# Sliding-window attention followed by a gated feed-forward layer: a smaller first weight load, batch 0's small steps in another order, and value casts by head into the tile layout

## The chip, the cores and the metric

The kernel runs on one core of a Trainium2 chip. The metric is device time in microseconds (us), as the median of several runs. Five engines of the core work side by side, each on its own queue in its own order: TensorE (PE, matrix products; PEld is its weight load), VectorE (DVE), ScalarE (ACT), GpSimd (POOL) and SyncE (SP). Transfers between HBM and the on-chip memory are issued from POOL's queue or from SP's queue and are carried by 16 DMA engines that all queues share.

## The reference

Eight batches of eight heads, 576 tokens and 64 values per head go through attention in which a query sees the keys within 32 positions, and 8 global tokens see and are seen by everything. The result, laid out as 4608 tokens of 512 values, goes through a feed-forward layer whose nonlinearity is h + sin(alpha h)^2 / alpha.

```python
scores = scale * np.matmul(q, k.transpose(0, 1, 3, 2))
mask = np.abs(pos[:, None] - pos[None, :]) <= window      # window = 32
mask = mask | is_global[:, None] | is_global[None, :]
attn = softmax(np.where(mask, scores, -1e9))
x = (attn @ v).transpose(0, 2, 1, 3).reshape(B * S, H * D)
h = x @ w_in                                              # 512 -> 2048
s = np.sin(alpha * h)
out = (h + s * s / (alpha + 1e-9)) @ w_out                # 2048 -> 512
```

## The kernel before, in words

The order of the work on every engine is the order in which the code is written. The kernel goes through the batches with the attention of one batch beside the second product of the batch before: `phase_a(0)`, then for each batch b `gemm1(b)` (x @ w_in with the nonlinearity) and `phase_a(b + 1, b)`, in which the products of `gemm2(b)` (g @ w_out, line 1220) are spread by hand with `fill(n)` between the steps of batch b + 1's attention. `fill` has nothing to lay into batch 0's attention, which therefore runs alone; that is the start that the change touches.

**Batch 0's attention** is `first_batch` (called in `attention`). The eight heads go in four pairs hp = 0 to 3. For each pair `scores` (line 814) makes the scores in PSUM, ACT takes their exponential (line 822), DVE multiplies the mask in (`cover`, line 831). `denominators(hp)` is 28 matmuls with a weight of ones (line 862 into `zd`), then the logarithm on ACT (`L`, line 772, which writes the tile `L` and issues its copy to `LC` from SP), then a small sum for the global tokens on DVE (`GD`, line 756). `inverse(hp)` is exp(-L) on ACT (`R`, line 779). `first_numerators(hp)` is 28 matmuls with the values `VF` as weights (line 862), 8 for the global rows (line 878) and `normalise`: the product with `R` into `xT` (line 908) and the sum `GN` (line 756) on DVE. In batch 0 the numerators go to PSUM banks `zr` (hp 0 and 2), `zn` (hp 1) and `zd` (hp 3); the denominators of every pair go to `zd`. `set_recip` turns alpha into a column (a PE transpose, line 710, and a DVE copy, line 711) and makes 1/(alpha + 1e-9) from it (`recipT`, lines 712 and 713). `warm(z, n)` (line 569) is n matmuls of 512 columns whose result nobody reads.

In the kernel before, the pairs' loop ends with `denominators(2)`. Then follow on PE: numerators 0, numerators 1, the alpha transpose, denominators 3, numerators 2, one warm matmul, numerators 3, two warm matmuls, and `gemm1(0)`.

**`gemm1(0)`** goes through 16 groups nt of 128 columns of w_in (line 1115). It first makes the chunks 0 to 2 of groups 0 and 1 (which need xT of pairs 0 to 2), then chunk 3 of both, then whole groups. Three PSUM tiles, `zn`, `zr` and `zd`, take turns, so group 3 needs the tile of group 0 back: ACT's sine (line 1162, needs `alphaT`), a square (line 1165 on ACT or 1167 on DVE) and DVE's line 1168 (needs `recipT`) come between. Between the groups PE turns the keys and queries of batch 1 (`turn_lying`, line 630; `H` there is a corner of the tile H2 in which they lie) and the global keys and queries (`turn_kq`, line 726, from the two `gkq` tiles that POOL casts in line 717).

**POOL's queue** issues, in this order: the twelve loads of batch 0's values (line 392), `load_w_in(0, 1)` (line 426), a cast of the global values, a one-element copy (`pace`, line 353) that waits for the first exponential of pair 3, `load_w_in(1, 2)`, keys and queries of batch 1 for pairs 0 and 1 (line 456), `load_w_in(2, 4)`, the same for pairs 2 and 3, a copy that waits for the edge of the value tile, the cast of batch 1's values to a bf16 copy in HBM (`cast_v(1)`, line 334), the two halves of w_out (line 432), the two `gkq` casts, and the cast of batch 2's queries. `load_w_in(lo, hi)` counts quarters of w_in's 2048 columns. A transfer issued from POOL uses one of eight semaphores in turn (DMASW0 to DMASW7), and the instruction that issues it waits until the transfer eight places earlier has landed.

**SP's queue** gathers the global rows of v, k and q (lines 518 and 512), then writes batch 0's four logarithms to `LC`, then loads batch 1's values from their cast copy (`load_v(1)`, line 407, tile `VF`; `vd` is the cast copy), then the global rows beside them (line 414).

The cast copy `vd` of a batch has the layout [token, head, value]. A partition of the value tile takes one token of each of 7 key tiles of 48 tokens, so `load_v` reads 7 pieces of 512 bf16 values for each of 48 partitions, twice.

`cast_one(b, name, h)` casts one head of a later batch; keys go into a copy with the layout [token within a key tile, key tile, head, value] (line 344), queries and values into [token, head, value] (line 346).

Of the kernel before, what the change touches and what calls it, by code (L numbers as in the profile page):

```python
# [249 lines left out]
def kernel(  # L250
# [85 lines left out]
    def cast_one(b, name, h):  # L336

        src = {"qd": q, "kd": k, "vd": v}[name][b, h]
        tiles = name == "kd"
        if h == 0:  # L340
# [7 lines left out]
    def cast_v(b):  # L348
        cast_heads(b, v, "vd")

# [51 lines left out]
    def load_v(b):  # L402

        src = cast[b, "vd"][:].rearrange("(m a) h d -> a m (h d)", a=KT)
        for half in range(2):
            m0 = half * (NT6 - 1)
            nc.sync.dma_start(
                out=VX[b % 2][half * D : half * D + KT].rearrange("p m h d -> p m (h d)"),
                in_=src[:, m0 : m0 + NT6 + 1],
            )  # L410
# [12 lines left out]
    def load_w_in(lo, hi):  # L423
        if lo < hi:
            cols = slice(lo * DFF // 4, hi * DFF // 4)
            nc.gpsimd.dma_start(
# [281 lines left out]

    def set_recip():
        nc.tensor.transpose(out=zo[0][:, 0:NT], in_=arow[:], identity=idf[0:NT, 0:NT])  # L710
        nc.vector.tensor_copy(out=alphaT[:], in_=zo[0][:, 0:NT])
        nc.vector.tensor_scalar(out=recipT[:], in0=alphaT[:], scalar1=1e-9, scalar2=None, op0=ALU.add)  # L712
        nc.vector.reciprocal(out=recipT[:], in_=recipT[:])
# [68 lines left out]
    def attention(b, beside):  # L782
# [136 lines left out]
        def first_batch():  # L919

            for hp in range(NHP):
# [5 lines left out]
                if hp == last:  # L927
                    pace(Es[hp][0:1, 0, 0, 0:1])
                    load_w_in(1, 2)
                    for hps in (early, late):  # L930
                        for w in (1, 0):
                            load_lying(1, w, hps)
                        if hps == early:
                            load_w_in(2, 4)
                    for half in (1, 0):
# [5 lines left out]
                for g in range(2 * (hp > 0)):  # L941
                    cover(hp, g)
                if hp:
                    denominators(hp - 1)
            release_ring()
            for hp in range(2):
                inverse(hp)
                first_numerators(hp)
            set_recip()
            inverse(last - 1)  # L950
            denominators(last)
            first_numerators(last - 1)
            warm(zo[1], 1)
# [4 lines left out]
            warm(zo[1], 2)  # L958
            normalise(last)
            pair["after"].release()  # L960

# [435 lines left out]
```

## Time and profile before

| | us |
|---|---|
| median of 3 runs | 338.68 (338.3 to 339.26) |
| the profiled execution | 338.49 |
| its span, first to last instruction | 336.8 |
| PE busy | 316.2 |
| ACT busy | 277.1 |
| DVE busy | 255.9 |
| POOL busy | 143.7 |

The profile is of one execution. Its own time is 338.49 us; 1.7 us of that lie outside the span of 336.8 us. All times below are counted from the span's start. In a list of groups or of the timeline each row is: start, busy time, engine, line, operation, output<-inputs, shape, count, and in square brackets the idle time of the engine just before, with what ended it. "issue" there means that the engine waited for nothing that the profile shows. In the rows on DMA the last number is the time from issue to landing. In the rows on queues the numbers are packets, megabytes and the time of the packets as a share of 16 engines' time; packets overlap, so shares can exceed 100%.

### The profile page before, as it was taken

The numbers are of one execution on the slowest core, as the hardware profiler recorded it, in microseconds if no ns is written. First come the engines' busy times: TensorE is split into PE (matmuls) and PEld (weight loads), VectorE is DVE, ScalarE is ACT, GpSimd is POOL, SyncE is SP. The second block draws the span as 40 slices with busy tenths as digits, with TensorE's granted clock in tenths as the row PEclk, the third lists the DMA queues.
The fourth block names the chain that finished last, engine by engine and source line by source line (L and its number), as shares of the span: only waits on it lengthen the run. The fifth ranks groups of instructions, "written<-read, shape, count | busy, mean of one in ns | idle before, by whom it ended". The sixth has DMA issues, their size and how long they took to land.

```text
span 336.8 us, 11878 instructions
## 1 busy us (share of the span) xinstructions
PE 316.2 (94%) x4812; PEld 202.8 (60%) x4812; DVE 255.9 (76%) x488; ACT 277.1 (82%) x402; POOL 143.7 (43%) x296
## 2 busy tenths in 40 slices
PE   0778999999999999999999999999999999999993
PEld 0765765577556765667556755676567745665553
DVE  4885896887887788688877788778868888788930
ACT  6775888989998889988998889889898898889611
POOL 7983324349516670666355652487060000004500
PEclk9999999999999999999999999999999999999998
DMA  7999999999989998999969993899999311010232
GB/s 104 114 162 205 186 226 169 152 166 135 181 143 133 190 124 137 94 119 186 151 93 137 172 162 85 131 176 136 132 111 133 65 60 42 1 33 8 73 93 69
DMA packets 141942, 42.01 MB, mean 125 GB/s; under 512 B 126426, under 2 KB 136794, under 8 KB 141882
## 3 DMA queue, kind: packets, MB, share of 16 engines
q0 software_dynamic: 100096, 18.51, 71.1%
q1 hardware_dynamic: 41786, 22.69, 34.1%
q8 instruction: 38, 0.62, 0.8%
q14 instruction: 22, 0.18, 0.2%
HBM read 41.95 MB, written 20.77 MB: 186 GB/s over the span
## 4 chain that ended last, share of the span: by engine, by line
PE 87%; DVE 4%; ACT 3%; issue 2%; DMA 1%; POOL 1%; DVEq 0%; POOLq 0%
PE zo L1220 38%; PE zn L1115 14%; PE zr L1115 11%; PE zd L1115 10%; PE ring L814 4%; PE zd L862 4%; PE zn L862 2%; DVE H L1168 2%; DMA g0k<-in_k_dram,grow 1%; ACT sb L1162 1%; PE zn L814 1%; PE zr L862 1%; DVE recipT L712 1%; DVE s L1167 1%; PE zo L630 1%
## 5 line engine op out<-in xcount | busy, mean ns | idle before, releaser
L1220 PE MATMUL zo<-w_out,H 128*128 128x512 bf16 (+1 forms) x576 | 147.1, 377 | 0.3 <-DVE KX L637 0.3
L1115 PEld LDWEIGHTS <-w_in 128*128 128x128 bf16 x1024 | 100.1, 98 | 43.9 <-issue 8.3
L1220 PEld LDWEIGHTS <-H 128*128 128x128 bf16 x592 | 53.7, 98 | 46.2 <-issue 0.4
L1115 PE MATMUL zn<-xT,w_in 128*128 128x288 bf16 (+1 forms) x384 | 57.7, 290 | 1.6 <-DVE H L1168 1.4
L1115 PE MATMUL zr<-xT,w_in 128*128 128x288 bf16 x320 | 48.0, 288 | 0.3
L1168 DVE SCALAR_TENSOR_TENSOR H<-s,recipT,zn 128x576 bf16<-128x576 bf16 (+1 forms) x48 | 39.4, 822 | 10.4 <-ACT s L1165 6.5
L1162 ACT ACTIVATE sb<-zn,alphaT 128x576 bf16<-128x576 f32 (+1 forms) x48 | 35.7, 743 | 13.7 <-PE zn L1115 13.2
L1115 PE MATMUL zd<-xT,w_in 128*128 128x288 bf16 x320 | 46.3, 288 | 0.3 <-DVE H L1168 0.2
L822 ACT ACTIVATE E<-ring 128x720 bf16<-128x720 f32 x46 | 35.9, 780 | 8.3 <-PE ring L814 7.7
L1167 DVE TENSOR_TENSOR s<-sb 128x576 bf16<-128x576 bf16 (+1 forms) x70 | 32.6, 465 | 12.2 <-ACT sb L1162 12.0
L1165 ACT ACTIVATE s<-sb 128x576 bf16<-128x576 bf16 (+1 forms) x58 | 40.0, 689 | 1.8
L831 DVE TENSOR_TENSOR E<-E,MASKT 128x720 bf16<-128x720 bf16 x64 | 33.5, 529 | 7.6 <-ACT E L822 5.6
L1168 DVE SCALAR_TENSOR_TENSOR H<-s,recipT,zd 128x576 bf16<-128x576 bf16 (+1 forms) x40 | 32.9, 822 | 7.6 <-ACT s L1165 5.0
L1168 DVE SCALAR_TENSOR_TENSOR H<-s,recipT,zr 128x576 bf16<-128x576 bf16 (+1 forms) x40 | 32.9, 822 | 6.6 <-ACT s L1165 5.0
L344 POOL DMA_DIRECT2D kd<-in_k_dram x48 | 31.4, 657 | 10.4 <-issue 8.0
L1162 ACT ACTIVATE sb<-zd,alphaT 128x576 bf16<-128x576 f32 (+1 forms) x40 | 29.6, 740 | 5.2 <-PE zd L1115 5.1
L1162 ACT ACTIVATE sb<-zr,alphaT 128x576 bf16<-128x576 f32 (+1 forms) x40 | 29.6, 740 | 4.3 <-PE zr L1115 4.3
L1210 POOL COPY H<-H 128x11 bf16 (+1 forms) x16 | 7.2, 453 | 57.6 <-DVE H L1168 56.7
L346 POOL DMA_DIRECT2D vd<-in_v_dram x48 | 30.5, 645 | 1.7 <-issue 1.3
L346 POOL DMA_DIRECT2D qd<-in_q_dram x40 | 25.4, 635 | 6.0 <-issue 6.0
L1227 ACT COPY osb<-zo 128x512 f32<-128x512 f32 (+1 forms) x33 | 19.1, 580 | 10.6 <-PE zo L1220 7.0
L814 PEld LDWEIGHTS <-KX 64*64 64x64 bf16 x896 | 15.8, 112 | 19.4 <-issue 19.0
(171 smaller groups left out, 377.7 us busy)
## 6 DMA issues: line engine op xcount, KB each, us to landing
VF<-vd SPq DMA_DIRECT2D x14, 336.0 KB
kd<-in_k_dram POOLq DMA_DIRECT2D x48, 72.0 KB, 4.8
vd<-in_v_dram POOLq DMA_DIRECT2D x48, 72.0 KB, 4.1
qd<-in_q_dram POOLq DMA_DIRECT2D x40, 72.0 KB, 5.5
w_out<-in_moe_w_out_dram POOLq DMA_DIRECT2D x2, 1024.0 KB, 25.7
out_dram<-osb SPq DMA_DIRECT2D x7, 256.0 KB
out_dram<-osb SPq DMA_DIRECT2D x8, 224.0 KB
out_dram<-osb SPq DMA_DIRECT2D x8, 192.0 KB
```

The source lines that it names most:

```text
L344: nc.gpsimd.dma_start(out=dst[:, :, h], in_=src.rearrange("(i a) d -> a i d", a=KT))
L346: nc.gpsimd.dma_start(out=dst[:, h], in_=src)
L814: nc.tensor.matmul(out=z[half * D : (half + 1) * D, t, 0 : G3 * WCOL].rearrange("p (m x c) -> p m x c", x=2, c=60)[:, m % G3, :, c0:c1], l ...
L822: nc.scalar.activation(out=weights(hp, g), in_=z[:, :, 0 : G3 * WCOL], func=AF.Exp, scale=scale)
L831: nc.vector.tensor_tensor(out=Eg, in0=Eg, in1=MASKT[:, None, G3 * g : G3 * (g + 1), :].rearrange("p o m c -> p o (m c)").to_broadcast([P, ...
L862: nc.tensor.matmul(out=nd(hp, key)[t * D : (t + 1) * D, half, :, a - half * CUT : z - half * CUT], lhsT=ones[rows, 0:D] if key else values ...
L1115: nc.tensor.matmul(out=h_part, lhsT=w_in[:, c, nt * P : (nt + 1) * P], rhs=xT[:, c, lo:hi], start=(c == 0), stop=(c == CT - 1), skip_group ...
L1162: nc.scalar.activation(out=sb[:, 0:W], in_=h, func=AF.Sin, scale=alphaT[:, nt : nt + 1])
L1165: nc.scalar.activation(out=s2[:, 0:W], in_=sb[:, 0:W], func=AF.Square)
L1167: nc.vector.tensor_tensor(out=s2[:, 0:W], in0=sb[:, 0:W], in1=sb[:, 0:W], op=ALU.mult)
L1168: nc.vector.scalar_tensor_tensor(out=H2[:, nt, r0 : r0 + W], in0=s2[:, 0:W], scalar=recipT[:, nt : nt + 1], in1=h, op0=ALU.mult, op1=ALU.add,)
L1220: nc.tensor.matmul(out=ops[:, cols], lhsT=H2[:, nt, blk * P : (blk + 1) * P], rhs=w_out[:, nt, cols], start=(nt == 0), stop=(nt == NT - 1) ...
```

## The change

There are three edits. First, `load_w_in` counts eighths instead of quarters; the call `load_w_in(0, 1)`, whose line is the same, now loads the first eighth (256 columns, groups nt = 0 and 1), the second call loads the next three eighths and the third the upper half as before. Second, the small steps of batch 0 are put in another order: `set_recip` is split into `set_alpha` (transpose and copy) and a `set_recip` that is only the two DVE operations and comes behind the last `normalise`; `inverse(0)` comes before `denominators(2)`; `denominators(3)` comes before numerators 1 and 2 and behind one more warm matmul. Third, batch 1's values are cast by eight transfers of one head each, and the cast copy of the values of every batch takes the layout that the keys have, so that `load_v` finds the 7 pieces of a partition side by side.

```diff
-        tiles = name == "kd"
+        tiles = name != "qd"
...
     def cast_v(b):
-        cast_heads(b, v, "vd")
+        for h in range(H):
+            cast_one(b, "vd", h)
...
     def load_v(b):
-        src = cast[b, "vd"][:].rearrange("(m a) h d -> a m (h d)", a=KT)
+        src = cast[b, "vd"][:].rearrange("a m h d -> a m (h d)")
...
     def load_w_in(lo, hi):
-            cols = slice(lo * DFF // 4, hi * DFF // 4)
+            cols = slice(lo * DFF // 8, hi * DFF // 8)
...
-    def set_recip():
+    def set_alpha():
         nc.tensor.transpose(out=zo[0][:, 0:NT], in_=arow[:], identity=idf[0:NT, 0:NT])
         nc.vector.tensor_copy(out=alphaT[:], in_=zo[0][:, 0:NT])
+
+    def set_recip():
...
-                    load_w_in(1, 2)
+                    load_w_in(1, 4)
...
-                            load_w_in(2, 4)
+                            load_w_in(4, 8)
...
+                if hp == last:
+                    inverse(0)
                 if hp:
                     denominators(hp - 1)
             release_ring()
-            for hp in range(2):
-                inverse(hp)
-                first_numerators(hp)
-            set_recip()
-            inverse(last - 1)
+            inverse(1)
+            first_numerators(0)
+            set_alpha()
+            warm(zo[1], 1)
             denominators(last)
-            first_numerators(last - 1)
+            inverse(2)
+            first_numerators(1)
+            first_numerators(2)
             warm(zo[1], 1)
...
             normalise(last)
+            set_recip()
```

**DVE at the end of batch 0's attention, before.** xT is the normalised result, GN and GD are the sums for the global tokens, recipT is 1/(alpha + 1e-9):

```order
L908 TENSOR_TENSOR xT<-zr,R 128x576 [waits PE_49,Activation_49]
L756 TENSOR_REDUCE GN<-zr 128x2x4
L908 TENSOR_TENSOR xT<-zn,R 128x576 [waits PE_49,Activation_49]
L756 TENSOR_REDUCE GN<-zn 128x2x4
L711 COPY alphaT<-zo_125 128x16 [waits PE_49]
L712 TENSOR_SCALAR recipT<-alphaT 128x16 [waits DVE_49]
L713 RECIPROCAL recipT<-recipT 128x16 [waits DVE_49]
L756 TENSOR_REDUCE GD<-zd 128x2x4 [waits Activation_49]
L908 TENSOR_TENSOR xT<-zr,R 128x576 [waits PE_49]
L756 TENSOR_REDUCE GN<-zr 128x2x4
L908 TENSOR_TENSOR xT<-zd,R 128x576 [waits PE_49,Activation_49]
L756 TENSOR_REDUCE GN<-zd 128x2x4
```

The same place of the changed kernel, whose lines are numbered 3 higher here:

```order
L911 TENSOR_TENSOR xT<-zr,R 128x576 [waits PE_49]
L759 TENSOR_REDUCE GN<-zr 128x2x4
L712 COPY alphaT<-zo_125 128x16 [waits PE_49]
L759 TENSOR_REDUCE GD<-zd 128x2x4 [waits Activation_49]
L911 TENSOR_TENSOR xT<-zn,R 128x576 [waits PE_49]
L759 TENSOR_REDUCE GN<-zn 128x2x4
L911 TENSOR_TENSOR xT<-zr,R 128x576 [waits PE_49,Activation_49]
L759 TENSOR_REDUCE GN<-zr 128x2x4
L911 TENSOR_TENSOR xT<-zd,R 128x576 [waits PE_49,Activation_49]
L759 TENSOR_REDUCE GN<-zd 128x2x4
L715 TENSOR_SCALAR recipT<-alphaT 128x16 [waits DVE_49]
L716 RECIPROCAL recipT<-recipT 128x16 [waits DVE_49]
```

The sum GD of pair 3, for which PE's numerators 3 wait (they reuse zd), has moved ahead of pairs 1 and 2, and the two recipT operations have moved from before it to the end of the row. On PE, likewise, denominators 3 now stand behind the alpha transpose and a warm matmul and ahead of numerators 1 and 2.

**POOL's queue from the second w_in load to w_out, before.** H_97 is the place where batch 1's keys and queries lie, seen is the one-element copy:

```order
L426 DMA w_in<-in_moe_w_in_dram 128x4x512 [waits DMASW3_49]
L456 DMA H_97<-in_k_dram 48x4x768 [waits DMASW4_49]
L456 DMA H_97<-in_q_dram 48x4x768 [waits DMASW5_49]
L426 DMA w_in<-in_moe_w_in_dram 128x4x1024 [waits DMASW6_49]
L456 DMA H_97<-in_k_dram 48x4x768 [waits DMASW7_49]
L456 DMA H_97<-in_q_dram 48x4x768 [waits DMASW0_49]
L937 COPY seen<-VF_91 1x1 [waits DVE_49,Pool_49]
L334 DMA vd<-in_v_dram 4608x1x64 [waits DMASW1_49]
L432 DMA w_out<-in_moe_w_out_dram 128x8x512 [waits DMASW2_49]
L432 DMA w_out<-in_moe_w_out_dram 128x8x512 [waits DMASW3_49]
```

In the changed kernel the six loads ahead stand in the same places with the same semaphores, and behind them:

```order
L940 COPY seen<-VF_91 1x1 [waits DVE_49,Pool_49]
L344 DMA vd<-in_v_dram 576x1x64 [waits DMASW1_49]
L344 DMA vd<-in_v_dram 576x1x64 [waits DMASW2_49]
L344 DMA vd<-in_v_dram 576x1x64 [waits DMASW3_49]
L344 DMA vd<-in_v_dram 576x1x64 [waits DMASW4_49]
L344 DMA vd<-in_v_dram 576x1x64 [waits DMASW5_49]
L344 DMA vd<-in_v_dram 576x1x64 [waits DMASW6_49]
L344 DMA vd<-in_v_dram 576x1x64 [waits DMASW7_49]
L344 DMA vd<-in_v_dram 576x1x64 [waits DMASW0_49]
L433 DMA w_out<-in_moe_w_out_dram 128x8x512 [waits DMASW1_49]
L433 DMA w_out<-in_moe_w_out_dram 128x8x512 [waits DMASW2_49]
```

One cast has become eight, so the third to the eighth head now wait for the second w_in load, the four loads of batch 1's keys and queries and the third w_in load to land, and the two halves of w_out wait for the first and the second head's cast instead of for the first two w_in loads.

## The prediction

> **What bounds the kernel now.** I read the page first, then PE's waits behind the start, then PE's timeline in the start, since that is where the order of the small steps lies.
>
> ```profile
> span 336.8 us, 11878 instructions
> ```
> ```profile
> PE zn L1115 <- DVE H L1168: 1.4, 2, 1.0
> ```
> The second row is the largest of PE's waits after 30 us. PE is the bound from there to the end, so whatever the start gives back reaches the end, unless a transfer that doesn't come earlier takes it away. So there are two questions: how much earlier does `gemm1(0)` begin, and what is PE's next tight date? The timeline of PE answers the first:
>
> ```profile
> 15.23 0.38 PE L862 MATMUL zd<-E,ones 56*64 56x120 bf16 x9 [0.68 <-issue]
> ...
> 20.24 0.79 PE L862 MATMUL zd<-E,ones 56*64 56x88 bf16 x28
> ...
> 24.38 0.51 PE L862 MATMUL zd<-E,ones 56*64 56x120 bf16 x16 [1.02 <-issue]
> ...
> 26.78 0.79 PE L862 MATMUL zd<-E,VF 56*64 56x88 bf16 x28 [0.48 <-DVE GD L756]
> ...
> 27.77 1.03 PE L569 MATMUL zo<-ones 128*128 128x512 bf16 x2
> 28.60 1.65 PE L1115 MATMUL zn<-xT,w_in 128*128 128x288 bf16 x6
> 30.04 1.14 PE L1115 MATMUL zr<-xT,w_in 128*128 128x288 bf16 x6
> ...
> 31.50 1.14 PE L1115 MATMUL zd<-xT,w_in 128*128 128x288 bf16 x8
> 33.67 1.14 PE L1115 MATMUL zn<-xT,w_in 128*128 128x288 bf16 x8 [1.03 <-DVE H L1168]
> 34.65 1.14 PE L1115 MATMUL zr<-xT,w_in 128*128 128x288 bf16 x8
> ```
> From denominators 2 (20.24) to `gemm1(0)` (28.60) PE needs 8.36 us, and two gaps lie in them: 1.02 us in the middle of denominators 3, where no instruction is waited for, and 0.48 us ahead of numerators 3, for the sum GD on DVE. Beside the gaps there is pace: the six matmuls from 28.60 to 30.04 start every 240 ns, the eight from 33.67 to 34.65 every 123 ns. The first 16 of `gemm1(0)` take 2.90 us and would take 1.97 at the later pace.
>
> The tight date is found behind the start. The second half of w_out is used first here:
>
> ```profile
> 51.34 1.67 PE L1220 MATMUL zo<-w_out,H 128*128 128x512 bf16 x7 [0.25 <-DVE KX L637]
> ...
> 55.80 0.47 PE L862 MATMUL zd<-E,ones 56*64 56x88 bf16 x28
> ...
> 56.23 2.10 PE L1220 MATMUL zo<-w_out,H 128*128 128x512 bf16 x9
> ```
> and the halves are issued by POOL, and land after the time at the row's end (lists of one issue each):
>
> ```profile
> 25.48 1.34 POOL L432 DMA_DIRECT2D w_out<-in_moe_w_out_dram  x1
> 27.63 0.89 POOL L432 DMA_DIRECT2D w_out<-in_moe_w_out_dram  x1 [0.80 <-DMA w_in<-in_moe_w_in_dram]
> ```
> ```profile
> w_out<-in_moe_w_out_dram POOLq DMA_DIRECT2D x1, 1024.0 KB, 22.9
> ```
> ```profile
> w_out<-in_moe_w_out_dram POOLq DMA_DIRECT2D x1, 1024.0 KB, 28.6
> ```
> The first half lands at 25.48 + 22.9 = 48.4, 2.9 us before its use at 51.34. The second lands at 27.63 + 28.6 = 56.2, and PE begins with it at 56.23, straight behind denominators that began at 55.80. This date has no slack: a PE that comes earlier waits here for w_out, and the start's gain counts only as far as w_out's second half lands earlier too.
>
> **The order of the small steps.** GD of pair 3 comes late because of what stands ahead of it on DVE:
>
> ```profile
> 24.23 2.13 DVE L712 TENSOR_SCALAR recipT<-alphaT 128x16 f32<-128x16 f32 x1
> 26.40 0.25 DVE L713 RECIPROCAL recipT<-recipT 128x16 f32<-128x16 f32 x1
> ...
> 32.23 0.46 DVE L1167 TENSOR_TENSOR s<-sb 128x576 bf16<-128x576 bf16 x1 [3.37 <-ACT sb L1162]
> ```
> The change puts both directly ahead of line 1167, the last of these rows. Even at 2.13 + 0.25 = 2.38 us they fit into the 3.37 us in which DVE waits for ACT, so they cost nothing there; without that cover they would cost up to 2.38. GD now comes two numerators ahead of its use, which ends the 0.48 us. ACT makes R of pair 0 ahead of the logarithm of pair 2; what waits for that is GD of pair 2 and then denominators 3, which come later on PE by numerators 0 and a warm matmul, so I take nothing. The additional warm matmul costs half of what two take from 27.77 to 28.60: 0.41 us.
>
> The gap of 1.02 us is a load of code. The first row is POOL's transfer queue (q0) from 14 to 16 us, around the gap of 0.68 at 15.23; the other two are that queue and the instruction queue (q8) from 22 to 24 us, where one packet of code runs just ahead of the gap of 1.02:
>
> ```profile
> q0 software_dynamic: 1481, 0.18, 144.1%
> ```
> ```profile
> q0 software_dynamic: 318, 0.32, 104.1%
> ...
> q8 instruction: 1, 0.02, 3.0%
> ```
> The pieces in the queue are 0.18 MB / 1481 = 122 bytes ahead of the short gap and 1 KB ahead of the long one. If a code load stands behind the pieces of other queues, their size sets its wait. The first eighth has pieces of 512 bytes where the first quarter has 1 KB. So the gap is between 1.02 (it stays) and nothing; I take the half with the smaller pieces, 0.4 left.
>
> On the rings, the Trainium skill ("DMA: Bandwidth & Descriptors", Queues, rings and completion order) says that an engine drains a whole packet, typically 9 to 17 descriptors, of one ring before it turns to the next. By that rule the code load waits for some 16 pieces, half as long with pieces half as large; the two gaps agree in direction, and nothing here shows the count.
>
> So `gemm1(0)` begins earlier by 0.62 + 0.48 - 0.41 = 0.7 us (0.07 with the gap kept, 1.09 without it). If PE has its later pace by then, 2.90 - 1.97 = 0.93 more; the bounds of the gain are 0.07 and 2.02, and I take 1.3. What is late next is `zn` for group 3 (33.67), which hangs on group 0 and moves along.
>
> The Trainium skill ("TensorE: Matmul & The Clock Gate", What's actually happening) says that PE runs at half rate until it has been busy through one free-running window of about 3.4 us. By that rule the closed gaps bring the full rate a window earlier and the gain is 2.0 rather than 1.1; the trace agrees in that the pace doubles between 30.04 and 31.50, about 4 us behind the last gap.
>
> **The w_in split.** The bytes stay the same. Only the queue can run dry between the smaller first load and the second, whose issue waits for an exponential:
>
> ```profile
> 16.50 0.87 POOL L426 DMA_DIRECT2D w_in<-in_moe_w_in_dram  x1
> ...
> 19.88 0.76 POOL L426 DMA_DIRECT2D w_in<-in_moe_w_in_dram  x1
> ```
> ```profile
> w_in<-in_moe_w_in_dram POOLq DMA_DIRECT2D x1, 512.0 KB, 6.3
> ```
> Half of 6.3 us would land the eighth at 19.65; the next load is issued by 20.64. So the queue is empty for 0 to 1.0 us, and all that stands behind it, w_out last, comes later by as much. I take 0.3, since the queue still has values to carry when the eighth is issued.
>
> **The casts by head.** POOL pays eight issues for one:
>
> ```profile
> L344 POOL DMA_DIRECT2D kd<-in_k_dram x48 | 31.4, 657 | 10.4 <-issue 8.0
> ```
> ```profile
> 23.10 0.57 POOL L456 DMA_DIRECT2D H<-in_q_dram  x1
> ...
> 23.79 2.16 POOL L334 DMA_DIRECT2D vd<-in_v_dram  x1
> ```
> ```profile
> H<-in_q_dram POOLq DMA_DIRECT2D x1, 288.0 KB, 15.1
> ```
> ```profile
> vd<-in_v_dram POOLq DMA_DIRECT2D x1, 576.0 KB, 18.0
> ```
> Eight at 657 ns are 5.3 us for 2.16, but the waits weigh more. The eighth head waits for the last queries, 23.10 + 15.1 = 38.2, and w_out's halves for the first two heads. The cast of the values lands at 23.79 + 18.0 = 41.8 now, so it moves from 38.2 to 41.8, 0.45 us per head. The first head is then done by about 39, w_out is issued within another 1.34 us, and the queue has values until 41.8: it doesn't run empty. If landings are seen late, w_out comes up to 1 us late; I take 0.2. Behind w_out on POOL stand the `gkq` casts:
>
> ```profile
> 36.45 0.61 POOL L717 CAST gkq<-SQ 64x512 bf16<-64x512 f32 x1 [6.63 <-DMA LC<-L]
> ```
> ```profile
> 46.03 0.68 PE L726 MATMUL zo<-identb,gkq 64*64 64x32 bf16 x32
> ```
> Issued about 41.5, they end by 43, ahead of 46.03 less 1.3.
>
> What can bring w_out forward is the new layout. SP's load of the values runs beside w_out. The rows are POOL's queue from 42 to 45 us, alone, then both from 46 to 50:
>
> ```profile
> q0 software_dynamic: 588, 0.60, 121.7%
> ```
> ```profile
> q0 software_dynamic: 471, 0.48, 70.3%
> q1 hardware_dynamic: 470, 0.46, 48.5%
> ```
> ```profile
> VF<-vd SPq DMA_DIRECT2D x14, 336.0 KB
> ```
> Alone, w_out moves 588 / 3 = 196 packets per us; beside 470 packets of SP's it loses 784 - 471 = 313 in 4 us, so one of SP's costs 0.67 / 196 = 3.4 ns. The two loads of a batch are 672 packets of 1 KB: 2.3 us. As 96 packets of 7 KB they cost 0.3 us if the price is per packet, 2.3 if it is per byte. The gain is 0 to 2.0 us. Pieces of 122 bytes moved at 740 per us (1481 in 2 us), an eighth of the bytes at a quarter of the price, which is nearer to the byte; I take 0.8. The later batches' loads gain the same way, but PE waits for none of them.
>
> **The sum.** w_out's second half lands at 56.2 + 0.3 + 0.2 - 0.8 = 55.9. PE is ready for it at 56.2 - 1.3 = 54.9 and waits 1.0 us. Gain: 0.3 us of 338.49, the profiled execution's own time, which is 0.2 under the median of 338.68. That gives 338.2, and on the scale of the median 338.4; I say 338.2, as the gain has more room above than below. A measurement of this kernel can tell about 0.3%, 1.0 us, from no change.
>
> **Rivals.** Faster: the price is per packet, and w_out lands 1.0 us or more earlier, up to 56.2 - 2.0 = 54.2; then the start's 1.1 to 2.0 come through, and the time is 336.5 to 337.5, middle 337.0. For it: the two gaps on PE are real, and the new pieces are seven times larger. Against it: the packet prices above. Chance 0.36.
>
> Slower: POOL stands behind the eight semaphores and the queue runs dry ahead of w_out. A single head's cast takes this long by its row:
>
> ```profile
> kd<-in_k_dram POOLq DMA_DIRECT2D x48, 72.0 KB, 4.8
> ```
> Issued from 38.2 to 38.9, the eighth head would land at 43.7 instead of 41.8: 1.9 us. With 1.0 from the first load and no gain from the layout w_out's second half lands at 59.1. It decides from 57.2 on, where the loss passes 1.0 us, and gives 339.5 to 341.4, middle 340.4. Against it: the queue should still hold values when w_out is issued. Chance 0.17.
>
> The start doesn't get shorter: the code load comes as late as before, the gain is 0.07, and the time stays within 0.3% whatever w_out does up to 57.2. This and my forecast are the same verdict; together 0.47, of which the forecast has 0.3. The forecast's own range is 337.7 to 339.7. The whole range, with half of the fast rival's lower end and some of the slow one's, is 336.7 to 339.8.
>
> **What would show it.** Right: L1115 begins at 27.3 or so; the gap in front of it on GD is gone; a wait of about a microsecond on w_out stands at the first use of its second half, near 55.9; POOL waits on transfers between the heads. The order's part is wrong if the 1.02 us stay or the matmuls keep 240 ns to 30 us. The cap is wrong if w_out lands a microsecond or more ahead of 55.9, or behind 57.2. A wait of PE on `gkq`, on the second w_in load or on the values would be one that I cost at nothing.

## The result, and the profile after

| | before | after |
|---|---|---|
| median | 338.97 us (338.3 to 340.08, 4 runs) | 344.27 us (343.89 to 346.33, 4 runs) |
| the profiled execution, and its span | 338.49, 336.8 | 344.05, 342.4 |

The ratio is 1.0168, with a 95% interval of 1.0138 to 1.0197: slower by 1.7%, outside the predicted range of 336.7 to 339.8.

In the profiled execution the start comes earlier by about what the prediction said, though not by the way that it said. PE's timeline after:

```profile
24.73 0.35 PE L865 MATMUL zn<-E,VF 56*64 56x120 bf16 x9 [1.07 <-issue]
...
28.35 0.90 PE L1122 MATMUL zn<-xT,w_in 128*128 128x288 bf16 x6
...
30.31 1.14 PE L1122 MATMUL zd<-xT,w_in 128*128 128x288 bf16 x8
32.48 1.14 PE L1122 MATMUL zn<-xT,w_in 128*128 128x288 bf16 x8 [1.03 <-DVE H L1175]
```

The wait on GD is gone, the wait without a named releaser has stayed (1.07 us), and the six matmuls from 28.35 run at the full pace from the first one. Group 2 begins at 30.31 instead of 31.50: a gain of 1.2 us where 1.3 was forecast. Only 0.25 of it is an earlier begin (28.35 against 28.60); the rest is the pace. Twenty microseconds on, the same timeline has this:

```profile
54.91 0.61 PE L1227 MATMUL zo<-w_out,H 128*128 128x512 bf16 x1 [4.95 <-DMA w_out<-in_moe_w_out_dram]
55.74 2.34 PE L1227 MATMUL zo<-w_out,H 128*128 128x512 bf16 x5 [0.22 <-issue]
58.01 0.51 PE L817 MATMUL ring<-QX,KX 64*64 64x88 bf16 x14
...
61.64 2.12 PE L1227 MATMUL zo<-w_out,H 128*128 128x512 bf16 x8
```

PE stands for 4.95 us at the first half of w_out, not at the second. It was ready at 49.96, and the half lands at 54.9 instead of 48.4. The matmuls up to the next scores then take 3.10 us (54.91 to 58.01), where the same stretch took 1.60 before (51.34 to 52.94). The page's row of the granted clock (tenths of full speed, 40 slices of the span) shows a 6 in that slice:

```profile
PEclk9999996999999999999999999999999999999999
```

The second half lands at 59.9 and is used at 61.64 without a wait: the first half's delay hides it.

Why the first half is late stands in POOL's timeline:

```profile
23.30 1.33 POOL L344 DMA_DIRECT2D vd<-in_v_dram  x2
28.72 0.64 POOL L344 DMA_DIRECT2D vd<-in_v_dram  x1 [4.09 <-DMA w_in<-in_moe_w_in_dram]
...
37.45 0.64 POOL L344 DMA_DIRECT2D vd<-in_v_dram  x1 [4.55 <-DMA w_in<-in_moe_w_in_dram]
38.69 0.65 POOL L344 DMA_DIRECT2D vd<-in_v_dram  x1 [0.60 <-DMA H<-in_k_dram]
40.17 0.65 POOL L344 DMA_DIRECT2D vd<-in_v_dram  x1 [0.83 <-DMA H<-in_q_dram]
40.79 1.78 POOL L433 DMA_DIRECT2D w_out<-in_moe_w_out_dram  x2
42.56 1.18 POOL L720 CAST gkq<-SQ 64x512 bf16<-64x512 f32 x2
```

From the third head on, each cast waits for the transfer eight places earlier, and w_out is issued at 40.79, fifteen microseconds later than before (25.48). Then the value load, issued by SP at 43.78, meets it. The shared queues from 48 to 52 us in the changed kernel (packets, megabytes, share):

```profile
q1 hardware_dynamic: 134, 0.58, 87.7%
q0 software_dynamic: 178, 0.18, 34.9%
```

w_out (q0) gets 178 packets in 4 us, where the kernel before moved 471 beside its value load. Alone it would have moved 784 (196 per us), so 606 packets, 3.1 us of w_out, are missing in the stretch in which the pieces of 7 KB run.

How a delay builds up can be seen by comparing the start of the same ScalarE instruction in two traces. Each row is one instruction: its start before, then how much later (or, negative, earlier) it starts in the other runs, which are described below.

```
before  order  order_  heads_old  large_pieces  after  order_    cast_
        _only  split   _layout    _one_cast            and_cast  only
 31.46  -1.61  -1.89    -2.38       -3.84       -1.20   -0.37    -0.20
 48.61  -1.61  -1.68    -2.38       -3.55       -1.19   -0.05     0.05
 53.35  -1.62   1.30     0.62        3.01        5.23    3.98     6.07
 59.61  -0.47   1.79     3.02        3.99        5.43    4.23     6.87
 66.73  -0.20   2.03     3.43        4.17        5.51    4.31     6.93
313.75   0.07   2.06     3.58        5.86        6.07    4.31     7.90
```

All that matters happens between 48 and 63 us, where PE takes up w_out; what stands there afterwards reaches the end nearly unchanged (some runs lose 0.5 to 1.6 us more near 98 us). For the changed kernel the jump is 6.6 us: 4.95 of waiting, 1.5 for the matmuls at half the pace (3.10 us against 1.60), and small remainders.

### The profile page after: what moved, and what is told of

The parts are those of the page before. It is cut to its first block, busy times and chain, and to the rows that moved or that the text cites. A ratio compares the mean times of both kernels' runs of the same rounds, so it can differ in the third digit from the quotient of the medians.

```text
span 342.4 us, 11832 instructions
## 1 busy us (share of the span) xinstructions
PE 310.9 (91%) x4754; PEld 202.7 (59%) x4813; DVE 254.4 (74%) x488; ACT 276.8 (81%) x402; POOL 146.3 (43%) x303
## 4 chain that ended last, share of the span: by engine, by line
PE 79%; DMA 11%; issue 3%; DVE 2%; POOL 2%; ACT 2%; POOLq 0%; DVEq 0%
PE zo L1227 35%; PE zn L1122 13%; PE zd L1122 9%; PE zr L1122 9%; DMA H<-in_q_dram 6%; DMA w_out<-in_moe_w_out_dram 4%; PE ring L817 4%; PE zd L865 3%; PE zn L865 2%; DVE H L1175 1%; ACT sb L1169 1%; PE zn L817 1%; POOL H L457 1%; PE zr L865 1%; PE zd L1271 1%
## 5 line engine op out<-in xcount | busy, mean ns | idle before, releaser
L1227 PE MATMUL zo<-w_out,H 128*128 128x512 bf16 (+1 forms) x517 | 135.6, 379 | 10.9 <-issue 5.3
L1227 PEld LDWEIGHTS <-H 128*128 128x128 bf16 x592 | 53.8, 98 | 51.8 <-DMA w_out<-in_moe_w_out_dram 5.3
L1122 PE MATMUL zn<-xT,w_in 128*128 128x288 bf16 (+1 forms) x384 | 56.9, 287 | 2.2 <-DVE H L1175 1.4
L344 POOL DMA_DIRECT2D vd<-in_v_dram x56 | 37.3, 699 | 14.4 <-DMA w_in<-in_moe_w_in_dram 8.6
L1217 POOL COPY H<-H 128x11 bf16 (+1 forms) x16 | 7.2, 452 | 57.5 <-DVE H L1175 56.6
```

The lines of the kernel that those rows point to most:

```text
L344: nc.gpsimd.dma_start(out=dst[:, :, h], in_=src.rearrange("(i a) d -> a i d", a=KT))
L1122: nc.tensor.matmul(out=h_part, lhsT=w_in[:, c, nt * P : (nt + 1) * P], rhs=xT[:, c, lo:hi], start=(c == 0), stop=(c == CT - 1), skip_group ...
L1227: nc.tensor.matmul(out=ops[:, cols], lhsT=H2[:, nt, blk * P : (blk + 1) * P], rhs=w_out[:, nt, cols], start=(nt == 0), stop=(nt == NT - 1) ...
```

## The experiments

Theory: w_out's first half is late because the eight casts hold its issue back, because the large pieces then run ahead of it, and because the smaller first load leaves a hole in the queue. Rivals: one of these alone makes the loss; or the new order of the small steps does. Each ratio below is of medians; each row is of one profiled execution.

**The parts alone.** `order_only` is the kernel before with the second edit alone (the diff is that of `set_alpha`, `inverse`, `warm` and `denominators` above).

> The kernel before with the second edit alone (the new order of batch 0's small steps). If the loss comes from w_out's transfers alone, the third group of gemm1(0) begins near 30.3 instead of 31.50, PE reaches w_out's first half near 50.1, finds it there (48.4), and waits about 1.2 us for the second half, which lands at 56.2 as before: 338 to 339 us, ratio 0.997 to 1.000. If the new order itself costs something behind the start, which the gain at its beginning hides, the ratio is above 1.003 with no wait for w_out in it. If the quicker start came from the smaller first load and not from the order, the third group begins at 31.5.

Measured: 338.89 us beside 339.21, ratio 1.0001 (0.9979 to 1.0022). The cap was where the prediction put it:

```profile
29.90 1.14 PE L1121 MATMUL zd<-xT,w_in 128*128 128x288 bf16 x8
...
56.03 2.10 PE L1226 MATMUL zo<-w_out,H 128*128 128x512 bf16 x9 [1.38 <-DMA w_out<-in_moe_w_out_dram]
```

Group 2 is 1.6 us earlier, and 1.38 of that are spent waiting for w_out's second half.

`order_split` adds the first edit:

```diff
-            cols = slice(lo * DFF // 4, hi * DFF // 4)
+            cols = slice(lo * DFF // 8, hi * DFF // 8)
-                    load_w_in(1, 2)
+                    load_w_in(1, 4)
-                            load_w_in(2, 4)
+                            load_w_in(4, 8)
```

> The first and second edits (smaller first load, new order), batch 1's values in one cast in the old layout. If the first load's bubble of 1.7 us simply moves all that stands behind it, w_out's first half lands at 50.1 and the second at 57.9, PE waits 2.9 us for the second half, and the time is 340.3 to 340.8 (ratio 1.004 to 1.006). Rival: the smaller first load alone makes the loss: 343 or more, PE waits 4 us or more for the first half. Rival: the bubble is made up for, since nothing else uses the queue: 338 to 339.

Measured: 341.11, ratio 1.0049 (1.0024 to 1.0074), the expected ratio (1.004 to 1.006), but the wait is at the first half and not at the second:

```profile
51.53 2.61 PE L1226 MATMUL zo<-w_out,H 128*128 128x512 bf16 x7 [2.03 <-DMA w_out<-in_moe_w_out_dram]
```

The hole is plain in POOL's queue (q0) from 20 to 22 us, first in `order_only`, then in `order_split`:

```profile
q0 software_dynamic: 331, 0.32, 111.8%
```
```profile
q0 software_dynamic: 65, 0.06, 53.9%
```

0.26 MB are missing; at the 0.20 MB per us that w_out has when alone (0.60 MB in 3 us) that is 1.3 us. Taken to 23 us it is 0.48 against 0.15 MB, or 1.6 us: the queue is still thin for two microseconds behind the issue of the second load (19.87 to 20.63). w_out's first half lands at 51.5, 3.1 us later than without the split; why 1.6 us grow to 3.1 isn't shown.

`cast_only` is the kernel before with the third edit alone:

```diff
-        tiles = name == "kd"
+        tiles = name != "qd"
-        cast_heads(b, v, "vd")
+        for h in range(H):
+            cast_one(b, "vd", h)
-        src = cast[b, "vd"][:].rearrange("(m a) h d -> a m (h d)", a=KT)
+        src = cast[b, "vd"][:].rearrange("a m h d -> a m (h d)")
```

> The kernel before with the third edit alone (eight casts, new layout). No bubble in the queue, so the last queries land at 38.2 and w_out is issued at about 39; the thin queue and the large pieces then put w_out's first half at 52.5 to 53.5, and PE, with the old start, wants it at 51.3 and waits 1.2 to 2.2 us; the second half lands at 58 to 58.5 where PE wants it at 58: 341 to 342.5 us (ratio 1.006 to 1.010). Rival: without the bubble everything comes in time: 338.5 to 339.5. Rival: the third edit alone makes the whole loss: 344.

Measured: 344.19, ratio 1.0121 (1.0082 to 1.0160). The expectation was too low; the rival that the third edit alone makes nearly all of the loss holds:

```profile
55.75 0.61 PE L1221 MATMUL zo<-w_out,H 128*128 128x512 bf16 x1 [4.62 <-DMA w_out<-in_moe_w_out_dram]
```

In this execution the last queries landed two microseconds later than I had counted, so w_out was issued at 41.05 instead of 39.

`order_and_cast` is the changed kernel with the first load at its old size.

> The changed kernel with the first load at its old size (second and third edits). If the smaller first load costs about 1.7 us at w_out's dates, these come that much earlier than in the changed kernel: first half at 52.5 to 53.5, PE waits some 3 us for it: 342 to 343.2 us (ratio 1.008 to 1.012). Rival: the smaller first load costs nothing once the casts are late: 344 as in the changed kernel.

Measured: 343.72, ratio 1.0143 (1.0105 to 1.0180), a little above the expectation, and a wait of 2.96 us for the first half at 53.98. The changed kernel has 1.0168 (1.0138 to 1.0197): the intervals overlap, so beside the casts the split's part is not resolved, though its place (54.9 against 54.0) has the expected sign.

**Inside the third edit.** `heads_old_layout` is the changed kernel with the eight casts and the old layout:

```diff
-        tiles = name != "qd"
+        tiles = name == "kd"
-        src = cast[b, "vd"][:].rearrange("a m h d -> a m (h d)")
+        src = cast[b, "vd"][:].rearrange("(m a) h d -> a m (h d)", a=KT)
```

> The changed kernel with the eight casts, but with the old layout of the cast copy, so that the value load keeps its 1 KB pieces. If issue order and value load each bear part of the loss: w_out's first packet near 42.4, the first half lands at 50 to 51.5, PE waits 0 to 1.5 us for it, the second half lands near 58.5: 340.8 to 342 us (ratio 1.006 to 1.010). Rival: the late issue behind the eight semaphores is the whole cause: 344 (1.016), first half at 54 or later. Rival: it is only the large pieces: as with one cast, 340.5.

`large_pieces_one_cast` is `order_split` with another view of the old layout, which gives pieces of 7 KB but puts other tokens into the value tile:

```diff
-        src = cast[b, "vd"][:].rearrange("(m a) h d -> a m (h d)", a=KT)
+        src = cast[b, "vd"][:].rearrange("(a m) h d -> a m (h d)", a=KT)
```

> The first and second edits and one cast, but the value load reads 7 KB that lie side by side in the old layout, so the value tile holds other tokens and the output is not the reference's. It has the changed kernel's large pieces without its eight casts. If the large pieces take the engines from w_out's first half for about 4 us instead of about 2 later: first half lands at 52 to 53, PE waits 2 to 3 us for it and starts again at half pace: 342 to 343.5 (ratio 1.010 to 1.014). Rival: the pieces cost nothing beside the same bytes in 1 KB: the same time as with one cast and small pieces, 340.5.

Measured: 341.82, ratio 1.0089 (1.0054 to 1.0123), and 343.98, ratio 1.0127 (1.0087 to 1.0167), both ratios as expected; PE's waits for the first half are longer than expected (2.84 us for 0 to 1.5, 5.05 for 2 to 3). First the heads' waits, then the large pieces':

```profile
51.95 1.69 PE L1227 MATMUL zo<-w_out,H 128*128 128x512 bf16 x7 [2.84 <-DMA w_out<-in_moe_w_out_dram]
...
59.52 2.10 PE L1227 MATMUL zo<-w_out,H 128*128 128x512 bf16 x9 [2.63 <-DMA w_out<-in_moe_w_out_dram]
```
```profile
52.68 3.17 PE L1226 MATMUL zo<-w_out,H 128*128 128x512 bf16 x7 [5.05 <-DMA w_out<-in_moe_w_out_dram]
```

and the queues from 48 to 52 us in the same two kernels, pieces of 1 KB and then of 7 KB:

```profile
q0 software_dynamic: 479, 0.47, 70.1%
q1 hardware_dynamic: 482, 0.48, 46.4%
```
```profile
q1 hardware_dynamic: 118, 0.40, 81.3%
q0 software_dynamic: 214, 0.22, 48.7%
```

With pieces of 1 KB the two queues share the engines about evenly, 0.48 to 0.47 MB; with 7 KB the value load takes nearly two thirds of the bytes, and w_out gets less than half of its packets. While the large pieces run, from 48 to 50 us, the two queues still move about as many packets each, 55 (q0) to 54 (q1), but 0.06 to 0.29 MB. Against `order_split` (51.5) the heads alone put w_out's first half at 51.9 and the pieces alone at 52.7; both together put it at 54.9. By these single executions they are more than the sum. That fits w_out, issued late, falling behind the load that lets it through least; the two runs that follow, which undo one of them each, bear it out. In time the pieces cost some 0.8% with one cast (1.0127 against 1.0049) and with eight (1.0168 against 1.0089). The heads' 0.4% are not resolved either time, since the intervals overlap.

**Undoing one part in the changed kernel.** `values_held` lets SP read one element of w_out's first half before it loads the values:

```diff
+                nc.sync.dma_start(out=held[:], in_=w_out[0:1, 0, 0:1])
                 load_v(1)
```

> The changed kernel, in which one element of w_out's first half is read by SP ahead of batch 1's value load, so that the large pieces start only when that half has landed. If the value load takes the engines from w_out's first half, that half lands near 50.3 instead of 54.9 and PE waits less than 1 us for it. The pieces then run beside the second half, which lands near 59.9 as in the changed kernel; PE wants it at about 55.5, waits some 4 us there, and has it 1.7 us before the 61.64 at which it took it up in the changed kernel: 342 to 343 us (ratio 1.009 to 1.012). Rival: the late issue alone makes the date, so the first half still lands at 54 or later: 344.

`first_half_between` issues w_out's first half behind the second head:

```diff
         for h in range(H):
+            if h == 2:
+                load_w_out((0,))
             cast_one(b, "vd", h)
...
-                    load_w_out((0, 1))
+                    load_w_out((1,))
```

> The changed kernel, in which the first half of w_out is issued behind the second head's cast and the other six heads behind it. If the late issue costs w_out's first half its date, it now lands at about 46, before PE wants it at 50, and that wait is gone. The value load comes behind the heads, at 49 to 53, and beside the second half, which lands near 57; PE wants it at 55: a wait of 2 us there, 339.5 to 341 us (ratio 1.002 to 1.006). Rival: what counts is all that the queue carries, so an earlier first half only makes the second later, at 59.9: 342.5 or more.

Measured: 344.35, ratio 1.0131 (1.0085 to 1.0177), and 342.69, ratio 1.0090 (1.0061 to 1.0120). In both PE's wait for the first half is gone, as the theory has it. First `values_held`, then `first_half_between`:

```profile
51.76 1.69 PE L1229 MATMUL zo<-w_out,H 128*128 128x512 bf16 x6 [1.14 <-DVE H L1177]
...
57.91 2.10 PE L1229 MATMUL zo<-w_out,H 128*128 128x512 bf16 x8 [1.20 <-DMA w_out<-in_moe_w_out_dram]
62.09 0.23 PE L866 MATMUL zn<-E,VF 56*64 56x88 bf16 x2 [1.80 <-DMA VF<-VGb]
62.74 0.49 PE L866 MATMUL zn<-E,VF 56*64 56x88 bf16 x26 [0.42 <-DMA VF<-VGb]
```
```profile
30.45 1.15 PE L1124 MATMUL zd<-xT,w_in 128*128 128x288 bf16 x8 [1.92 <-DMA w_in<-in_moe_w_in_dram]
...
52.34 1.67 PE L1229 MATMUL zo<-w_out,H 128*128 128x512 bf16 x6
...
58.27 2.10 PE L1229 MATMUL zo<-w_out,H 128*128 128x512 bf16 x8 [0.99 <-DMA w_out<-in_moe_w_out_dram]
```

But holding the values back gained nothing: PE then waits for w_out's second half (1.20 us) and for the value tile (1.80 and 0.42), a date that I had left out, its clock is halved from 63.8 to 67.2, and the total missed its expectation by 1.4 us. With the first half between the heads the profiled execution took 340.54 us, within the expectation; the median does not, and lies where the rival had it (342.5 or more); the runs reach from 339.92 to 343.68. What its other executions waited for is not shown. So the date of 54.9 takes both, the late issue and the large pieces: with either undone PE begins with w_out at 51.8 or 52.3. Taking the wait away doesn't give the time back, though. The row of `first_half_between` at 30.45 shows one more price of the smaller first load: PE waits 1.92 us for the second load of w_in. `order_split` shows it too, with 0.86 us at group 2 and 0.52 at the first group of the upper half; in the changed kernel's profiled execution PE doesn't wait there.

**Can the order's gain reach the end?** `order_v_between` is `order_only` with w_out's first half ahead of the one value cast, and `order_v_behind` has both halves ahead of it:

```diff
-                    cast_v(1)
-                    load_w_out((0, 1))
+                    load_w_out((0,))
+                    cast_v(1)
+                    load_w_out((1,))
```

> The kernel before with the new order of the small steps, and w_out's first half issued ahead of batch 1's value cast (one cast, old layout), the second half behind it. If the second half of w_out is what keeps the order's gain from the end, and the value load beside it is what makes it late: first half lands near 44.8, the cast near 48.4, value load 48.8 to 54, second half at 54 to 54.5, PE wants it at 54.7 to 55. No wait for w_out, the values are there before 57: 337 to 338 us (ratio 0.994 to 0.997). Rival: the second half lands at 56 as before, since the same bytes stand ahead of it: no change, 1.000. Rival: the values come late: over 1.000 with a wait on them.

> The same, with both halves of w_out ahead of the value cast. w_out lands at 44.8 and about 50, the cast at 53.6, and the value load runs from 54 beside the cast of batch 2's queries to 58 or later; PE wants the values at about 57. If the values become the date: PE waits 1 to 3 us for them, 338.5 to 340 us (ratio 0.999 to 1.004). Rival: the value load finishes in time, and the gain of the order comes through: 337 to 338.

Measured: 339.05, ratio 0.9986 (0.9963 to 1.0009), and 343.24, ratio 1.0102 (1.0063 to 1.0141). Both are above their expectations (337 to 338, and 338.5 to 340). The rows of the first, then of the second:

```profile
54.77 2.12 PE L1227 MATMUL zo<-w_out,H 128*128 128x512 bf16 x8
57.49 0.23 PE L864 MATMUL zn<-E,VF 56*64 56x88 bf16 x2 [0.33 <-DMA VF<-VGb]
...
60.56 0.21 PE L864 MATMUL zd<-E,ones 56*64 56x32 bf16 x3 [0.42 <-issue]
```
```profile
61.98 0.98 PE L864 MATMUL zn<-E,VF 56*64 56x88 bf16 x28 [4.90 <-DMA VF<-VGb]
```

w_out is in time in both; now the value tile is the date (VGb are its global rows, loaded last), by a little in the first and by 4.90 us in the second. Next, two things were moved out of the values' way. `order_q_later` is `order_v_between` with the cast of batch 2's queries behind the landing of batch 1's values:

```diff
-                cast_heads(2, q, "qd")
...
                     place_globals(1, part, nc.gpsimd.tensor_copy)
+                pace(VX[1][0:1, 0, 0, 0:1])
+                cast_heads(2, q, "qd")
```

> The run with the value cast between w_out's halves, and the cast of batch 2's queries issued only when batch 1's values have landed, so that the value load has the engines to itself behind w_out. If the values were the next date there, they land by 55 instead of 57.5, PE waits for neither w_out nor values, and the start's 1.4 us reach the end: 337.2 to 338 us (ratio 0.994 to 0.997). Rival: batch 2's queries become the date (their transpose ends after 66, wanted near 68): 339 or more. Rival: the gain is lost elsewhere between 57 and 63: 1.000.

`q_later_old_order` has the same transfers with the small steps as before.

> The same arrangement of the transfers with the small steps in their old order. In the kernel before PE waits for no transfer behind 30 us, so earlier transfers give it nothing: 338.5 to 339.3 us (ratio 0.998 to 1.002). Rival: the gain of the run beside it comes from the transfers and not from the order: 337.2 to 338 here too.

Measured: 344.85, ratio 1.0147 (1.0112 to 1.0181), and 344.52, ratio 1.0155 (1.0121 to 1.0189). The first is where its rival had it (the queries become the date), the second missed. PE waits for neither w_out nor values, and batch 2's queries are the date, on DVE, behind which PE waits 4.49 us at 75.73 in the first. DVE's row in the first, then in the second:

```profile
73.56 0.83 DVE L366 COPY QX<-qt 128x1152 bf16<-128x1152 bf16 x2 [4.97 <-DMA qt<-qd]
```
```profile
71.87 0.83 DVE L366 COPY QX<-qt 128x1152 bf16<-128x1152 bf16 x2 [2.47 <-DMA qt<-qd]
```

I had expected no change from the second, since PE waited for no transfer before; that a transfer that nobody waits for has little room was the mistake. Last, `order_rows_first` leaves the queries and loads the tile's global rows ahead of the values:

```diff
-                load_v(1)
-                load_vg(1)
+                load_vg(1)
+                load_v(1)
```

> The run with the value cast between w_out's halves, and the global rows loaded into the value tile ahead of batch 1's values instead of behind them. In that run PE waited for the global rows at 57.5 to 57.9, and 1.4 us of lead were lost between 59 and 63. If the last transfer into the value tile is what holds the order's gain back, the lead stays at 0.7 to 1.4 us behind 63 us: 337.3 to 338.4 us (ratio 0.994 to 0.998). Rival: the values themselves land as late as the rows did, and the lead is gone as before: 338.5 to 339.2 (0.998 to 1.001).

`rows_first_old_order` is the same in the old order, and `order_v_between_2` repeats the run above on the same chip.

> The same transfers with the small steps in their old order. PE waits for no transfer in the kernel before, so nothing is gained: 338.5 to 339.3 us (0.998 to 1.002), and the difference to the run beside it is what the new order is worth when no transfer stands in its way: 0.7 to 1.6 us. Rival: the rearranged transfers alone give it: 337.3 to 338.4 here too.

> The value cast between w_out's halves with the new order, again, beside the two: 338.4 to 339.2 us (0.997 to 1.001) if the values' date holds as it did.

Measured: 339.14, ratio 0.9996 (0.9978 to 1.0014); 339.51, ratio 1.0000 (0.9983 to 1.0017); 339.13, ratio 0.9997 (0.9979 to 1.0016). No version beats the kernel before by more than can be measured. `order_rows_first` missed its 337.3 to 338.4, and its difference to the old order is 0.4 us where 0.7 to 1.6 was expected; the rival, that the lead is lost as before, fits. Its profiled execution has no lead to lose, though:

```profile
28.18 1.65 PE L1122 MATMUL zn<-xT,w_in 128*128 128x288 bf16 x6
...
31.49 1.14 PE L1122 MATMUL zd<-xT,w_in 128*128 128x288 bf16 x8
```

`gemm1(0)` begins 0.4 us earlier than in the kernel before, but its first six matmuls run at half the pace, and group 2 begins at 31.49 where it began at 31.50. The repeat reached 59 us with a lead of 1.2 us and lost it here:

```profile
60.56 0.21 PE L864 MATMUL zd<-E,ones 56*64 56x32 bf16 x3 [0.99 <-issue]
```

That looks like a wait for code again. The instruction queue's packet begins at 58.0, 58.1, 58.6 and 59.0 in four of these kernels (`order_v_between_2`, `order_v_between`, `order_rows_first`, `rows_first_old_order`), and PE goes on at 60.56, 60.56, 61.23 and 61.43, 2.4 to 2.6 us later each time. In the kernel before it begins at 58.0 too, and PE comes to that place at about 60.5 and doesn't wait. What sets the beginning of that packet isn't shown. So w_out's second half (56.2), the values (57.5 in `order_v_between`) and this code (60.5) stand one behind the other without slack for a lead of 1.2 us, and each takes what the one before has left. For the code this is argued from the agreement of the four times; no run moved it alone.

## Why the prediction was wrong

- **The start: the number right, in part by luck.** Forecast 1.3 us, measured 1.2 in the profiled execution. The wait on GD ended and the reciprocals cost nothing where they went. But the 1.02 us of code load stayed (1.07), where 0.4 had been taken; by the prediction's own sign that part was wrong. `gemm1(0)` began 0.25 us earlier instead of 0.7, and the pace gave its full 0.94 instead of the 0.6 that the forecast took of it: two misses that cancelled. Nor does the new order fix the pace. Thirteen profiled executions with it are 0.02 to 3.84 us ahead at the start of the first group's sine, beyond the forecast's bounds of 0.07 to 2.02. `order_only` and `order_rows_first` have the same order on PE and begin `gemm1(0)` at 27.93 and 28.18, but the first 16 matmuls take 1.96 us in the one and 3.31 in the other, and the leads are 1.61 and 0.02 us.
- **The cap at w_out's second half: right for the order alone.** `order_only` waits there for 1.38 us and gains nothing. This cap is the first of the dates that take the order's lead; the value tile and, as argued above, the code follow.
- **"The first half lands at 48.4, 2.9 us before its use": the date that failed.** This step decided the miss. The first half was read as safe with a slack of 2.9 us, and delays were added up at the second half alone. It came 6.5 us later, and PE was ready for it 1.1 us earlier (49.96; before, it was ready at 51.09). The cost was worked out at one use of the transfer that was delayed, not at the first.
- **"The queue doesn't run empty, I take 0.2": failed.** w_out was issued at 40.79, and POOL's queue had little left to carry by then. Its row from 42 to 44 us, first before, then after:

```profile
q0 software_dynamic: 399, 0.41, 122.2%
```
```profile
q0 software_dynamic: 633, 0.17, 119.1%
```

  In packets it was busy, with the small pieces of the last heads; in bytes it moved less than half. The prediction's slow rival had this mechanism, with 1.9 us and a time of 340.4; `heads_old_layout`, nearest to it, measured 341.82. What it lacked was what follows from the late issue: w_out falls behind the value load on engines that both share.
- **"What can bring w_out forward is the new layout, I take 0.8": failed in sign.** It was priced as a saving, 0 to 2.0 us, by two rates of packets. `large_pieces_one_cast` shows a loss of some 0.8% instead: the two queues move about as many packets each while both run (54 to 55 from 48 to 50 us), so a piece of 1 KB gets through for a piece of 7 KB. A price per packet or per byte says what a load costs when its bytes are all that counts, not who gets the engines first.
- **The w_in split: mechanism right, size wrong.** 0.3 of at most 1.0 us was taken; the hole was 1.6 us of transfers. The sum let it end with the issue of the second load, and the queue stayed thin behind that: 0.07 MB from 20.7 to 22.5 us, against 0.25 without the split. w_out's first half came 3.1 us later in `order_split`.
- **The restart was not in the sum.** A wait of 4.95 us cost 6.6, mostly since PE came back at half its pace. The Trainium skill ("TensorE: Matmul & The Clock Gate", What's actually happening) has PE fall back to half rate after an idle window of about 3.4 us. The runs agree for waits of 4.95 and 5.05 us (six or seven matmuls in 3.1 us), and `heads_old_layout`, after 2.84 us, restarts at full pace (1.69 us for seven). But `order_split` is slow after only 2.03 us (2.61 us for seven). Two stretches of `order_split`, then two of `heads_old_layout`, show why; in each row stand the stretch, its length, the busy time and (behind x) the instructions of PE, PEld, DVE, ACT and POOL, then the granted clock:

```profile
48.73:52.14 3.41, 1.38 (x10) 0.70 (x8) 2.96 (x5) 2.90 (x4) 0.00 (x0) 1.00 1.17 239
52.14:55.55 3.41, 3.41 (x35) 1.41 (x34) 0.10 (x1) 0.90 (x2) 0.00 (x0) 0.50 1.36 212
```
```profile
47.40:50.81 3.41, 1.59 (x12) 0.89 (x10) 3.23 (x6) 2.96 (x5) 0.22 (x1) 1.00 1.17 242
50.81:54.22 3.41, 2.27 (x36) 1.12 (x37) 0.67 (x1) 0.71 (x2) 0.00 (x0) 1.00 1.22 217
```

  In `order_split` the clock is still full when PE starts again at 51.53; it halves at 52.14 and comes back at 55.55, 3.41 us later. The whole wait lies in the 3.41 us before the drop, of which PE was still busy for 1.38: less than a whole idle window was enough here, other than the Trainium skill says. In `heads_old_layout` the longer wait (49.11 to 51.95) falls on both sides of 50.81, and neither window is as empty. (50.81 is counted from that trace's own changes of the clock in steps of 3.41 us.) What share of a window makes the clock drop isn't settled by these runs.

The large change of transfers and the small change of order were made together. By the runs the order is worth nothing measurable (1.0001) with the transfers as they were, the third edit alone costs 1.2% and with the order 1.4%, and the first edit 0.5% where the casts are left alone.

## What to carry to other kernels

When a change delays a transfer, check it at its first use, with the slack that is left once the engine itself comes earlier, and with all that will then run beside it. Several loads that share the engines are one queue: in this kernel w_out's two halves, the values, the next queries and even code are due within 20 us, and moving one only chose which of them PE waits for. A wait of several microseconds on PE can cost more than its length: 4.95 us cost 6.6 here.

## What the runs showed of the hardware

- Two queues on the same DMA engines share them by pieces rather than by bytes. From 48 to 50 us they move 240 to 240 packets when both have 1 KB (`heads_old_layout`), and 70 (0.07 MB) to 67 (0.37 MB) when one has pieces of 7 KB (the changed kernel). The Trainium skill ("DMA: Bandwidth & Descriptors", Queues, rings and completion order) says that an engine drains one packet of several descriptors of a ring before it turns to the next; the traces fit turns of as many pieces from each queue, whatever their size, and don't show how many pieces a turn has.
- The clock of PE drops and recovers in steps of 3.41 us: every stretch at half clock between 40 and 90 us in the profiled executions lasts 3.41 or 6.83 us. A wait of 2.03 us brought one (`order_split`), a wait of 2.84 us brought none (`heads_old_layout`).
- The gap of about 1 us in PE's start goes with a code load. In the nine of 17 profiled executions that have a gap of 0.5 us or more it stands at one place for each order (behind 12 matmuls of denominators 3 in the old, behind 19 of numerators 1 in the new), and PE goes on 1.3 to 1.6 us after the end of the instruction queue's packet. In none of the 17 does PE pass that place earlier than 1.28 us behind that end. With the split's hole in the queue the packet begins at 20.4 to 21.6 us and five of six executions have no gap; without it, it begins at 21.6 to 22.5, and eight of eleven have one, up to 2.39. The changed kernel's own execution kept its gap although its packet began at 21.6: the packet took 1.7 us, where 0.9 to 1.2 is usual, and ended as late as in the runs without the split (23.2). That PE waits for this packet is argued from the agreement of these times; no run moved it alone.
